# Expert tables of 208 rows, and layer two of six experts with stationary weights

## The chip, the core and the metric

The kernel runs on one core of a Trainium2 chip. Time is device microseconds of one execution. The kernel before takes 768.36 us (median of three runs, 767.66 to 768.78). Engines: TensorE (PE, with weight loads shown apart as PEld), VectorE (DVE), ScalarE (ACT), GpSimd (POOL) and SyncE (SP), which issues most transfers.

## The reference, cut to what matters

Three layers follow each other: masked attention, a dense gated layer, and a routed layer. The change touches only the routed one:

```python
def _moe2_ref(x, w_skip, w_gate, w1, w2):       # x: 2304 tokens x 512
    do_compute = x @ w_skip > 0
    out = x.copy()
    xc = x[do_compute]
    logits = xc @ w_gate                        # 8 experts
    e_idx = np.argmax(logits, axis=1)
    gate_w = softmax(logits)[chosen]
    for e in range(8):
        mask = e_idx == e
        h = np.maximum(xc[mask] @ w1[e], 0.0)   # 512 -> 1024
        y[mask] = gate_w[mask, None] * (h @ w2[e])   # 1024 -> 512
    out[do_compute] = xc + y
```

## The kernel before

Attention, the dense layer (lines 541 to 592 hold most of its matmuls) and the routing fill the first 560 us or so. The routing writes every token row to `out` and scatters the rows of the chosen tokens into a table in DRAM, `xs`, which has SLOTS rows for each expert. An expert with more tokens would be finished by the pass at line 1395, a loop over 128 further rows whose bounds are read from the counts. Expert 0 has its first HEAD = 128 rows processed early: when the tokens of the last two units are ranked, its count is lifted to 128 at least (line 945).

Precision: float32 values are split into a high part (rounded to the engine's fp32r form) and a low part (the rest). A product is high x high + high x low + low x high, each a matmul that runs in fp32r.

All instructions of the span are issued in the order in which the program writes them; each engine runs its own in that order and waits by semaphores. For each of experts 1 to 7 (loop at line 1365):

1. `fetch` issues the loads of the next expert's table rows, `grab` one load of its weights. Weights come in eight pieces of 512 KB (four of w1, four of w2) through a pool of four raw buffers. A `settle` flushes the low part that the piece before left to do, issues a load, and casts a piece on ACT (line 1053). The low part of a w1 piece is POOL's, of a w2 piece DVE's (line 1054; expert 1's pieces alternate). A raw buffer is free, and its next load can be issued, once both parts are made.
2. Hidden stage: eight blocks f, `hidden_wide`. The weights are stationary (128 x 128), the moving side is the token rows transposed, high and low side by side: 448 columns for the high weights, 224 for the low ones, four such pairs a block, into one PSUM bank. Then ACT copies the second half to SBUF (line 1271), DVE adds it to the first (1273), and one block later ACT makes the relu's high part (1277) and DVE its low part (1281). Blocks take banks X and Y in turn, three of each. After every odd block stands a `settle`.
3. `prep` turns the next expert's rows with eight PE transposes (line 1110), in two parts of 128 and SLOTS - 128 rows, each in an X bank, and ACT and DVE make high and low parts (1112, 1114).
4. Layer two: `outputs` once for each part. The tokens are now stationary (128 or 96 columns) and w2 moves, 512 columns, 24 matmuls for a part (lines 1295, 1296, 1300, 1304), into one of two Z banks. DVE multiplies the bank with the gate and adds the row (1306), and POOL scatters the rows to `out` (1307). Two `settle`s stand in each part.

Of the kernel before, what the change touches and what calls it, by code (L numbers as in the profile page):

```python
# [10 lines left out]
F32R = mybir.dt.float32r  # L11
# [3 lines left out]
ALU = mybir.AluOpType  # L15
# [6 lines left out]
def kernel(  # L22
# [14 lines left out]
    nc = tc.nc  # L37
    B, H, S, D = q.shape
    NT, DM = out.shape
# [5 lines left out]
    KD = DM // 128  # L45
# [3 lines left out]
    NF = F // 128  # L49
    WQ = 96  # L50
    NW = S // WQ
    TW = DM + NE + 1
    SLOTS = 224
    HEAD = 128
    RB = 128
    UT = 384
# [30 lines left out]
    def temp(name):  # L87
        return keep.tile([128, UT], F32, tag="t", bufs=NT1, name=name)
# [3 lines left out]

    xs = dram.tile([NE * SLOTS, TW], F32, name="xs")
    vcm = dram.tile([B, S, 4 * D], F32, name="vcm")
# [6 lines left out]
    ident = const.tile([128, 128], F32, name="ident")  # L101
# [13 lines left out]
    def late_consts(i):  # L115
# [12 lines left out]
        if i == KD + 1:  # L128
            nc.gpsimd.iota(desc, pattern=[[-1, NE]], base=NE, channel_multiplier=0, allow_small_or_imprecise_dtypes=True)
            nc.gpsimd.iota(e_off, pattern=[[SLOTS, NE]], base=-int(OOB), channel_multiplier=0, allow_small_or_imprecise_dtypes=True)  # L130
            nc.gpsimd.memset(base_e, 0.0)
# [7 lines left out]
    def bank(shape, tag):  # L139
        return psum[0].tile(shape, F32, tag=tag, bufs=psum[1][tag], name="ps" + tag)  # L140
# [781 lines left out]
    def slab2(shape, dt, name):  # L922
        return late.tile(shape, dt, tag="slab2", bufs=NSLAB2, name=name)
# [133 lines left out]
    after_act = []  # L1057

    def flush(jobs):
        todo = list(jobs)  # L1060
        jobs.clear()
        for job in todo:
            job()

    w_e0, pp = [], []
# [10 lines left out]

    PARTS = ((0, HEAD), (HEAD, SLOTS))

# [22 lines left out]
    def prep(e, xg, parts=PARTS, xx=None, tag="X", gates=True, warm=0):  # L1101
        if xx is None:
            xx = [slab2([128, 2, 2, SLOTS], F32R, f"xx{e}{i}") for i in range(2)]
            xx.append(small.tile([128, 2, 2], F32, tag="gw", bufs=2, name="gw"))
        for a, c in parts:
            t, n = a // HEAD, c - a
            pt = bank([128, KD, n], tag)
            spin(warm, pt)
            for kk in range(KD):
                nc.tensor.transpose(pt[:, kk, :], xg[t][:n, 128 * kk:128 * kk + 128], ident[:n, :n])  # L1110
            for i in range(2):
                nc.scalar.copy(xx[i][:, :, 0, a:c], pt[:, 2 * i:2 * i + 2, :])
            for i in range(2):
                nc.vector.tensor_tensor(
                    xx[i][:, :, 1, a:c], pt[:, 2 * i:2 * i + 2, :], xx[i][:, :, 0, a:c].bitcast(F32), op=ALU.subtract)
            if gates:
                gate(xg, xx, a, c)
        return xx
# [79 lines left out]
    for u in range(NU):  # L1198
        po = [bank([128, UT], "X") for d in range(KD)]
        for f in range(NC):  # L1200
            i = u * NC + f
            ahead(i)
            for d in range(KD):
                ds_ = slice(128 * d, 128 * d + 128)
# [12 lines left out]
    pending, jobs = [], []  # L1217
    xg = head["xg"]

    def hidden(f, w, xx, hts, a=0, c=SLOTS, warm=0):  # L1220
        if f % 4 == 0 and len(hts) <= f // 4:
            hts.append([slab2([128, 4, SLOTS], F32R, f"h{n}{f}") for n in "hl"])
        n = c - a
        ph = bank([128, 2, n], "Y")
        spin(warm, ph)
        fs = slice(128 * f, 128 * f + 128)
        for kk in range(KD):
            xk = xx[kk // 2][:, kk % 2]
            nc.tensor.matmul(ph, lhsT=w[kk][0][:, fs], rhs=xk[:, :, a:c], start=(kk == 0), stop=(kk == KD - 1))
            if kk + 1 < KD:  # L1230
                nc.tensor.matmul(ph[:, 0, :], lhsT=w[kk][1][:, fs], rhs=xk[:, 0, a:c], start=False, stop=False)
            if kk + 2 == KD:
                nc.tensor.matmul(
                    ph[:, 0, :], lhsT=w[kk + 1][1][:, fs], rhs=xx[1][:, 1, 0, a:c], start=False, stop=False)
        hh, hl = (x[:, f % 4, a:c] for x in hts[f // 4])

        def evict():
            flush(pending)
            hs = temp("hs")[:, 0:n]
            nc.scalar.copy(hs, ph[:, 1, :])  # L1240
            flush(jobs)
            nc.vector.tensor_tensor(hs, hs, ph[:, 0, :], op=ALU.add)

            def finish():
                nc.scalar.activation(hh, hs, AF.Relu)
                jobs.append(low_part)

            def low_part():
                nc.vector.scalar_tensor_tensor(
                    hl, in0=hs, scalar=0.0, in1=hh.bitcast(F32), op0=ALU.max, op1=ALU.subtract)  # L1250

            pending.append(finish)

        return evict

    def hidden_wide(f, w, xx, hts):
        if f % 4 == 0:
            hts.append([slab2([128, 4, SLOTS], F32R, f"h{n}{f}") for n in "hl"])
        ph = bank([128, 2, SLOTS], "XY"[f % 2])
        total, rest = ph[:, 0, :], ph[:, 1, :]  # L1260
        fs = slice(128 * f, 128 * f + 128)
        for kk in range(KD):
            xk = xx[kk // 2][:, kk % 2]
            if kk == KD - 1:
                nc.tensor.matmul(total, lhsT=w[kk][1][:, fs], rhs=xk[:, 0, :], start=False, stop=False)
            nc.tensor.matmul(ph, lhsT=w[kk][0][:, fs], rhs=xk, start=(kk == 0), stop=(kk == KD - 1))
            if kk < KD - 1:
                nc.tensor.matmul(total, lhsT=w[kk][1][:, fs], rhs=xk[:, 0, :], start=False, stop=False)
        hh, hl = (x[:, f % 4, :] for x in hts[f // 4])
        hs = temp("hs")[:, 0:SLOTS]  # L1270
        nc.scalar.copy(hs, rest)
        flush(pending)
        nc.vector.tensor_tensor(total, total, hs, op=ALU.add)
        flush(jobs)

        def finish():
            nc.scalar.activation(hh, total, AF.Relu)
            jobs.append(low_part)

        def low_part():  # L1280
            nc.vector.scalar_tensor_tensor(
                hl, in0=total, scalar=0.0, in1=hh.bitcast(F32), op0=ALU.max, op1=ALU.subtract)

        pending.append(finish)

    def outputs(a, c, w, hts, xg, xx, between):
        t, n = a // HEAD, c - a
        flush(pending)
        flush(jobs)
        py = bank([n, DM], "Z")  # L1290
        hl_w2 = []
        for f in range(NF):
            hh, hl = (x[:, f % 4, a:c] for x in hts[f // 4])
            w2h, w2l = (x[:, f % 2, :] for x in w[4 + f // 2])
            nc.tensor.matmul(py, lhsT=hh, rhs=w2h, start=(f == 0), stop=False)
            nc.tensor.matmul(py, lhsT=hh, rhs=w2l, start=False, stop=False)
            hl_w2.append((hl, w2h))
            if f > 1:
                x, y = hl_w2.pop(0)
                nc.tensor.matmul(py, lhsT=x, rhs=y, start=False, stop=False)  # L1300
            if f in (2, 5):
                between()
        for x, y in hl_w2:
            nc.tensor.matmul(py, lhsT=x, rhs=y, start=False, stop=(y is w2h))
        y = xg[t][:n, 0:DM]
        nc.vector.scalar_tensor_tensor(y, in0=py, scalar=xx[2][:n, t, 1:2], in1=y, op0=ALU.mult, op1=ALU.add)
        nc.gpsimd.indirect_dma_start(  # L1307
            out=out[:, :], out_offset=bass.IndirectOffsetOnAxis(ap=xg[t][:n, TW - 1:TW].bitcast(I32), axis=0),
            in_=y, in_offset=None, bounds_check=NT - 1, oob_is_err=False,
        )  # L1310

    w = w_e0
    more, raws_e, wn, hts = True, [], [], []
# [14 lines left out]
    nxt = 1  # L1328
# [22 lines left out]
    xgn = fetch(1)[0]  # L1351
    outputs(0, HEAD, w, hts, xg, pp, idle)
    prep(0, xg, PARTS[1:], pp, warm=6)
    for f in range(NF):
        hidden(f, w, pp, hts, HEAD, SLOTS, 0 if f else 8)()
        if f == 5:
            ppn = prep(1, xgn)
# [4 lines left out]
        settle()  # L1362
    flush(after_act)
    w, xg, pp = wn, xgn, ppn
    for e in range(1, NE):
        nxt = e + 1
        more = nxt < NE
        raws_e, wn, hts = [], [], []
        if more:
            xgn = fetch(nxt)[0]  # L1370
        grab()
        for f in range(NF):
            hidden_wide(f, w, pp, hts)
            if f % 2:
                settle()
        ppn = prep(nxt, xgn) if more else None
        for a, c in PARTS:
            outputs(a, c, w, hts, xg, pp, settle)
        flush(after_act)
        if more:  # L1380
            w, xg, pp = wn, xgn, ppn
    manual.__exit__(None, None, None)

    cnt = const.tile([1, 1], F32, name="cnt")
# [10 lines left out]
    with tc.For_i(SLOTS, top, 128):  # L1395
# [32 lines left out]
        for e in range(NE):  # L1428
# [21 lines left out]
            for kk in range(KD):  # L1450
                t = slab([128, F], F32, f"ow1{e}{kk}")
# [3 lines left out]
            for i in range(NF // 2):  # L1455
                t = slab([128, 2, DM], F32, f"ow2{e}{i}")
# [3 lines left out]
            for f in range(NF):  # L1460
                ph = bank([128, 128], "Y")
                for kk in range(KD):
                    nc.tensor.matmul(
                        ph, lhsT=w1[kk][:, 128 * f:128 * f + 128], rhs=xT[:, kk, :], start=(kk == 0), stop=(kk == KD - 1)
                    )
                nc.scalar.activation(hT[:, f, :], ph, AF.Relu)
            py = bank([128, DM], "Z")
# [36 lines left out]
```

## Time and profile before

| | us |
|---|---|
| median of the runs | 768.36 |
| the profiled execution | 770.95 |
| its span, first to last instruction | 769.2 |
| PE busy | 738.8 (96%) |
| DVE busy | 505.7 (66%) |
| ACT busy | 400.3 (52%) |
| POOL busy | 210.4 (27%) |

Matmuls overlap in the records: one starts before the end of the one before it. So what a matmul costs a busy PE is the distance to the next start, and not its own duration.

### The profile page before, as it was taken

To read this page: it belongs to the slowest core of one execution; us is meant where nothing else is said; L and a number is where in the kernel's file an instruction comes from. 1 tells how busy PE (TensorE), PEld (TensorE's weight loads), DVE (VectorE), ACT (ScalarE), POOL (GpSimd) and SP (SyncE) were. 2 spreads that over 40 slices of the span, in tenths; PEclk is the share of its full clock that TensorE was granted. 3 is DMA by queue.
4 is the path that set the end of the run, shared out by engine and by line. 5 is a ranking of instruction groups with operands and counts; after the bars stand their busy time and mean duration, and the time that the engine had idled before them with its cause. 6 is when DMAs were issued, how large, how long until landed. Compare 5 with 4: busy or idle time off the path is not lost. (4 is left out here: it accounts for less than half of the span.)

```text
span 769.2 us, 13922 instructions
## 1 busy us (share of the span) xinstructions
PE 738.8 (96%) x4773; PEld 674.8 (88%) x4773; DVE 505.7 (66%) x1169; ACT 400.3 (52%) x1123; POOL 210.4 (27%) x233
## 2 busy tenths in 40 slices
PE   8899998999999999999999999999999999999993
PEld 5666766899999999999999999999999888888882
DVE  4599998789877777888764244345554666656550
ACT  5678886745444444444363233244444665567630
POOL 6468778000000000000010020120213755556510
PEclk9999999999999999999999999999989999999997
DMA  7888530063443344434383943536633667776600
GB/s 170 215 195 208 142 91 29 32 199 105 143 153 129 134 135 147 153 119 141 120 292 125 297 137 124 189 113 216 222 132 122 215 235 263 233 237 205 219 19 15
DMA packets 116309, 122.50 MB, mean 159 GB/s; under 512 B 58679, under 2 KB 91191, under 8 KB 116232
## 3 DMA queue, kind: packets, MB, share of 16 engines
q1 hardware_dynamic: 110504, 109.88, 46.1%
q0 software_dynamic: 4000, 8.51, 3.1%
q10 hardware_dynamic: 1728, 3.15, 1.1%
q8 instruction: 40, 0.66, 0.4%
q14 instruction: 37, 0.30, 0.1%
HBM read 90.78 MB, written 36.59 MB: 166 GB/s over the span
## 5 line engine op out<-in xcount | busy, mean ns | idle before, releaser
L541 PE MATMUL psX<-gt,wo 128*128 128x384 f32 x288 | 98.4, 342 | 1.0 <-DVE sl L1127 1.0
L542 PE MATMUL psX<-gt,wo 128*128 128x384 f32 x288 | 96.5, 335 | 0.1
L543 PE MATMUL psX<-gt,wo 128*128 128x384 f32 x288 | 96.4, 335 | 0.0
L592 POOL DMA_DIRECT2D gt<-sC x3 | 1.7, 566 | 256.4 <-DVE sC L590 256.4
L295 ACT ACTIVATE sm<-psX,mx 96x128 f32<-96x128 f32 (+2 forms) x176 | 62.0, 376 | 17.1 <-DVE mx L289 15.1
L308 POOL TENSOR_TENSOR sm<-sm,rs 96x384 f32<-96x384 f32 (+2 forms) x64 | 54.7, 873 | 38.5 <-DVE rs L302 26.7
L587 DVE TENSOR_TENSOR u<-psD,u 128x384 f32<-128x384 f32 x70 | 38.8, 554 | 29.0 <-PE psD L543 27.4
L541 PEld LDWEIGHTS psX<-gt,wo 128*128 128x128 f32 x288 | 54.2, 188 | 1.3 <-DVE sl L1127 1.3
L542 PEld LDWEIGHTS psX<-gt,wo 128*128 128x128 f32 x288 | 54.2, 188 | 0.4 <-DVE gt L857 0.4
L543 PEld LDWEIGHTS psX<-gt,wo 128*128 128x128 f32 x288 | 54.1, 188 | 0.0
L543 PE MATMUL psA<-xhB,wl 128*128 128x384 f32 x140 | 47.0, 336 | 0.7 <-DVE wl L514 0.7
L543 PE MATMUL psD<-xhT,wl 128*128 128x384 f32 x140 | 47.0, 336 | 0.3 <-DVE wl L514 0.3
L541 PE MATMUL psD<-xhT,wh 128*128 128x384 f32 x140 | 46.8, 335 | 0.0
L542 PE MATMUL psD<-xlT,wh 128*128 128x384 f32 x140 | 46.8, 334 | 0.0
L542 PE MATMUL psA<-xlB,wh 128*128 128x384 f32 x140 | 46.8, 334 | 0.0
L541 PE MATMUL psA<-xhB,wh 128*128 128x384 f32 x140 | 46.8, 334 | 0.0
L543 PE MATMUL psB<-xhT,wl 128*128 128x384 f32 x140 | 46.8, 334 | 0.0
L542 PE MATMUL psB<-xlT,wh 128*128 128x384 f32 x140 | 46.8, 334 | 0.0
L541 PE MATMUL psB<-xhT,wh 128*128 128x384 f32 x140 | 46.8, 334 | 0.0
L973 ACT COPY row<-psY 128x256 f32<-128x256 f32 x36 | 13.4, 373 | 62.2 <-PE psY L971 48.2
L974 DVE TENSOR_REDUCE lp<-psY 128x10 f32<-128x40 f32 x36 | 7.2, 200 | 56.6 <-ACT row L973 56.6
L580 ACT COPY psC<-psB 128x384 f32<-128x384 f32 x35 | 16.2, 464 | 51.6 <-PE psB L543 51.6
(764 smaller groups left out, 2263.1 us busy)
## 6 DMA issues: line engine op xcount, KB each, us to landing
w1r<-in_moe_w_dram SPq DMA_DIRECT2D x32, 512.0 KB, 5.2
w2r<-in_moe_w_dram SPq DMA_DIRECT2D x32, 512.0 KB, 3.8
gt<-gt SPq DMA_DIRECT2D x72, 192.0 KB, 3.8
gt<-sC SPq DMA_DIRECT2D x33, 192.0 KB, 2.5
gt<-sA SPq DMA_DIRECT2D x33, 192.0 KB, 1.9
wg<-in_moe_w_gate_dram SPq DMA_DIRECT2D x12, 512.0 KB, 4.0
wv<-in_moe_w_val_dram SPq DMA_DIRECT2D x12, 512.0 KB, 3.7
wo<-in_moe_w_out_dram SPq DMA_DIRECT2D x12, 512.0 KB, 3.8
```

The source lines that it names most:

```text
L295: nc.scalar.activation(sm[:n, w, 0:c], src[:, w, :], AF.Exp, bias=mx[:n, w:w + 1], accum_out=sums[:n, h, w:w + 1])
L308: nc.gpsimd.tensor_tensor(x, x, rs[:n, h, 0:m].rearrange("p (w o) -> p w o", o=1).to_broadcast([n, m, c]), op=ALU.mult)
L541: nc.tensor.matmul(ps, lhsT=whi, rhs=xhi, start=start, stop=False, skip_group_check=skip)
L542: nc.tensor.matmul(ps, lhsT=whi, rhs=xlo, start=False, stop=False, skip_group_check=skip)
L543: nc.tensor.matmul(ps, lhsT=wlo, rhs=xhi, start=False, stop=stop, skip_group_check=skip)
L580: nc.scalar.copy(ps, self.ps[src])
L587: nc.vector.tensor_tensor(self.tm[nm], self.ps["D"], self.tm[nm], op=ALU.add)
L592: eng.dma_start(gts[self.f][2 * self.p + i], self.tm[nm])
L973: nc.scalar.copy(row[m][:, 256 * a:256 * a + 256].rearrange("p (c n) -> p c n", c=2), pr[:, :, 0:128])
L974: nc.vector.tensor_reduce(lp[:, m, a, :], pr[:, :, 128:NR].rearrange("p c (t n) -> p n c t", t=2), axis=AX.XY, op=ALU.add)
```

## The change

SLOTS becomes 208. The parts of a table are then 128 and 80 rows, and the moving sides 416 and 208 columns. The hidden parts are kept differently: one tile for every two blocks holds the high and the low half of each block side by side, where there was a tile of four blocks for each half.

Experts 1 to 6 leave `outputs` for `outputs_wide`. For each quarter d of the 512 outputs, the w2 columns are stationary, high and low tokens move side by side (416 columns for the high weights, 208 for the low ones, eight pairs) into a Z bank; ACT copies the second half, DVE adds the first, and a `settle` follows. The four sums are outputs x tokens; `rows_back` turns them with eight PE transposes into two Y banks, and `store_rows` (the end of the former `outputs`) multiplies, adds and scatters. `rows_back` of an expert is called after block 0 of the next one. In these experts the last relu and low part are issued ahead of `prep`, and no longer behind it. Expert 0 and expert 7 keep `outputs`.

```diff
-    SLOTS = 224
+    SLOTS = 208
...
     def hidden_wide(f, w, xx, hts):
-        if f % 4 == 0:
-            hts.append([slab2([128, 4, SLOTS], F32R, f"h{n}{f}") for n in "hl"])
+        if f % 2 == 0:
+            hts.append(slab2([128, 2, 2, SLOTS], F32R, f"h{f}"))
...
-        hh, hl = (x[:, f % 4, :] for x in hts[f // 4])
+        hh, hl = (hts[f // 2][:, f % 2, i, :] for i in range(2))
...
+        store_rows(a, c, py, xg, xx)
+
+    def store_rows(a, c, py, xg, xx):
+        t, n = a // HEAD, c - a
         y = xg[t][:n, 0:DM]
         nc.vector.scalar_tensor_tensor(y, in0=py, scalar=xx[2][:n, t, 1:2], in1=y, op0=ALU.mult, op1=ALU.add)
         nc.gpsimd.indirect_dma_start(
...
+    def outputs_wide(w, hts, between):
+        ys = []
+        for d in range(KD):
+            ds_ = slice(128 * d, 128 * d + 128)
+            py = bank([128, 2, SLOTS], "Z")
+            total, rest = py[:, 0, :], py[:, 1, :]
+            for f in range(NF):
+                w2h, w2l = (x[:, f % 2, ds_] for x in w[4 + f // 2])
+                h = hts[f // 2][:, f % 2]
+                if f == NF - 1:
+                    nc.tensor.matmul(total, lhsT=w2l, rhs=h[:, 0, :], start=False, stop=False)
+                nc.tensor.matmul(py, lhsT=w2h, rhs=h, start=(f == 0), stop=(f == NF - 1))
+                if f < NF - 1:
+                    nc.tensor.matmul(total, lhsT=w2l, rhs=h[:, 0, :], start=False, stop=False)
+            y = temp("yT")[:, 0:SLOTS]
+            nc.scalar.copy(y, rest)
+            nc.vector.tensor_tensor(y, y, total, op=ALU.add)
+            ys.append(y)
+            between()
+        return ys
+
+    def rows_back(ys, xg, xx):
+        for a, c in PARTS:
+            py = bank([c - a, DM], "Y")
+            for d in range(KD):
+                nc.tensor.transpose(py[:, 128 * d:128 * d + 128], ys[d][:, a:c], ident)
+            store_rows(a, c, py, xg, xx)
...
             hidden_wide(f, w, pp, hts)
+            if f == 0 and left:
+                rows_back(*left)
             if f % 2:
                 settle()
-        ppn = prep(nxt, xgn) if more else None
-        for a, c in PARTS:
-            outputs(a, c, w, hts, xg, pp, settle)
-        flush(after_act)
         if more:
+            flush(pending)
+            flush(jobs)
+            ppn = prep(nxt, xgn)
+            left = outputs_wide(w, hts, settle), xg, pp
+            flush(after_act)
             w, xg, pp = wn, xgn, ppn
+        else:
+            for a, c in PARTS:
+                outputs(a, c, w, hts, xg, pp, settle)
```

## Rows read from the trace of the kernel before

**Rows 1.** The page: busy time of the engines; TensorE's granted clock in 40 slices.
```profile
PE 738.8 (96%) x4773; PEld 674.8 (88%) x4773; DVE 505.7 (66%) x1169; ACT 400.3 (52%) x1123; POOL 210.4 (27%) x233
...
PEclk9999999999999999999999999999989999999997
```

**Rows 2.** Stretches: length, busy time of each engine (instructions), clock, DMA share, GB/s.
```profile
670.60:692.50 21.90, 21.90 (x121) 18.70 (x120) 13.12 (x31) 13.62 (x32) 12.24 (x6) 1.00 0.71 236
```

**Rows 3.** PE in order of time, hidden block 1 of expert 4: start, duration, instruction.
```profile
671.04 0.36 PE L1266 MATMUL psY<-xx,we40h 128*128 128x448 f32 x1
671.23 0.26 PE L1268 MATMUL psY<-xx,we40l 128*128 128x224 f32 x1
671.33 0.38 PE L1266 MATMUL psY<-xx,we41h 128*128 128x448 f32 x1
```

**Rows 4.** PE in order of time: first instructions of the stages of expert 4.
```profile
669.76 0.37 PE L1266 MATMUL psX<-xx,we40h 128*128 128x448 f32 x1
...
679.81 0.93 PE L1110 MATMUL psX<-ident,xg 128*128 128x128 f32 x8
680.52 0.48 PE L1295 MATMUL psZ<-we44h,hh 128*128 128x512 f32 x1
...
686.17 0.39 PE L1295 MATMUL psZ<-we44h,hh 128*96 128x512 f32 x1
...
691.73 0.36 PE L1266 MATMUL psX<-xx,we50h 128*128 128x448 f32 x1
```

**Rows 5.** PE in order of time, expert 0: pairs of 256+128 and 192+96 columns.
```profile
565.98 0.34 PE L1229 MATMUL psY<-xx,we01h 128*128 128x256 f32 x1
...
566.21 0.34 PE L1229 MATMUL psY<-xx,we02h 128*128 128x256 f32 x1
...
589.39 0.32 PE L1229 MATMUL psY<-xx,we01h 128*128 128x192 f32 x1
...
589.62 0.32 PE L1229 MATMUL psY<-xx,we02h 128*128 128x192 f32 x1
```

**Rows 6.** PE in order of time, expert 1: the two turn-backs (brackets: idle before, releaser).
```profile
612.74 0.60 PE L1110 MATMUL psX<-ident,xg 128*128 128x128 f32 x4
614.28 0.55 PE L1110 MATMUL psX<-ident,xg 96*128 96x96 f32 x4 [0.94 <-DVE hl L1281]
```

**Rows 7.** ACT and DVE in order of time, expert 4.
```profile
671.23 0.35 ACT L1271 COPY hs<-psX 128x224 f32<-128x224 f32 x1 [4.32 <-PE psX L1266]
...
680.55 1.05 ACT L1053 CAST we53h<-w1r 128x1024 fp32r<-128x1024 f32 x1
...
688.12 1.05 ACT L1053 CAST we57h<-w2r 128x1024 fp32r<-128x1024 f32 x1 [1.79 <-DMA w2r<-in_moe_w_dram]
...
669.97 0.75 DVE L1306 SCALAR_TENSOR_TENSOR xg<-psZ,gw,xg 96x512 f32<-96x512 f32 x1 [2.55 <-PE psZ L1304]
670.63 1.21 DVE L1054 TENSOR_TENSOR we47l<-w2r,we47h 128x1024 fp32r<-128x1024 f32 x1
671.76 0.39 DVE L1273 TENSOR_TENSOR psX<-psX,hs 128x224 f32<-128x224 f32 x1
```

**Rows 8.** POOL in order of time, and DMA issues (KB each, us to landing).
```profile
674.11 2.40 POOL L1054 TENSOR_TENSOR we50l<-w1r,we50h 128x1024 fp32r<-128x1024 f32 x1 [1.13 <-ACT we50h L1053]
687.40 1.72 POOL L1307 DMA_INDIRECT out_dram<-xg  x1 [3.31 <-DVE xg L1306]
...
w1r<-in_moe_w_dram SPq DMA_DIRECT2D x16, 512.0 KB, 5.3
w2r<-in_moe_w_dram SPq DMA_DIRECT2D x16, 512.0 KB, 3.7
```

**Rows 9.** DVE and ACT in order of time, expert 1.
```profile
613.84 0.38 DVE L1281 SCALAR_TENSOR_TENSOR hl<-psX,hh 128x224 fp32r<-128x224 f32 x1
...
615.63 1.04 ACT L1053 CAST we23h<-w1r 128x1024 fp32r<-128x1024 f32 x1
...
625.39 1.06 ACT L1053 CAST we27h<-w2r 128x1024 fp32r<-128x1024 f32 x1 [2.64 <-DMA w2r<-in_moe_w_dram]
```

More of the change, by code (lines that the diff above doesn't have):

```diff
@@ L1220, in hidden @@
     def hidden(f, w, xx, hts, a=0, c=SLOTS, warm=0):
-        if f % 4 == 0 and len(hts) <= f // 4:
-            hts.append([slab2([128, 4, SLOTS], F32R, f"h{n}{f}") for n in "hl"])
+        if f % 2 == 0 and len(hts) <= f // 2:
+            hts.append(slab2([128, 2, 2, SLOTS], F32R, f"h{f}"))
         n = c - a
@@ L1234, in hidden @@
                     ph[:, 0, :], lhsT=w[kk + 1][1][:, fs], rhs=xx[1][:, 1, 0, a:c], start=False, stop=False)
-        hh, hl = (x[:, f % 4, a:c] for x in hts[f // 4])
+        hh, hl = (hts[f // 2][:, f % 2, i, a:c] for i in range(2))
         def evict():
@@ L1256, in hidden_wide @@
     def hidden_wide(f, w, xx, hts):
-        if f % 4 == 0:
-            hts.append([slab2([128, 4, SLOTS], F32R, f"h{n}{f}") for n in "hl"])
+        if f % 2 == 0:
+            hts.append(slab2([128, 2, 2, SLOTS], F32R, f"h{f}"))
         ph = bank([128, 2, SLOTS], "XY"[f % 2])
@@ L1286, in outputs @@
     def outputs(a, c, w, hts, xg, xx, between):
-        t, n = a // HEAD, c - a
+        n = c - a
         flush(pending)
@@ L1292, in outputs @@
         for f in range(NF):
-            hh, hl = (x[:, f % 4, a:c] for x in hts[f // 4])
+            hh, hl = (hts[f // 2][:, f % 2, i, a:c] for i in range(2))
             w2h, w2l = (x[:, f % 2, :] for x in w[4 + f // 2])
@@ L1364 @@
     w, xg, pp = wn, xgn, ppn
+    left = None
     for e in range(1, NE):
```

## The prediction

> **What bounds the kernel now.** I read the page first: TensorE (PE) is busy for 96% of the span, with 0.9 or more of the clock granted in all slices but two [rows 1]. The table of stretches then says which wait counts in the part that changes, experts 1 to 7: in a whole expert PE is busy in every microsecond at clock 1.00, while VectorE (DVE), ScalarE (ACT) and POOL fill 13.1, 13.6 and 12.2 us of 21.9, and DMA 0.71 of its share [rows 2]. So there the time is the sum of spacings between PE starts, as long as nothing makes PE wait; busy durations overlap and are not to be added. The order-of-time view of PE gives the spacings. In expert 4 the hidden stage runs from 669.76 to 679.81 (10.05 us), eight turn-back transposes to 680.52 (0.71), layer two to 691.73 (11.21): a period of 21.97 us [rows 4].
>
> **Price of a matmul.** One hidden block f lasts 10.05/8 = 1.256 us [rows 4]: four pairs of a 448-column and a 224-column matmul, 314 ns a pair, the wide one near 0.20, the narrow one 0.10 to 0.11 [rows 3]. A pair of 256+128 columns takes 0.23 us, one of 192+96 also 0.23 [rows 5]. So the short ones don't follow their columns: each matmul of new weights costs at least some 0.111 us. The 512-column matmuls of the second output part come every 5.56/24 = 0.2317 us [rows 4], 0.4525 ns a column. "Columns x 0.4525, but 0.111 at least" gives 314 for 448+224 (203+111), 227 for 256+128 and 222 for 192+96, as the rows have it within 8 ns. For 416+208 it gives 188+111 = **300 ns**. Bounds: 291 (the pair in proportion to columns) and 314 (no gain); the straight line between 230 at 384 columns and 314 at 672 also gives 300, which I take.
>
> The Trainium skill, TensorE: Matmul & The Clock Gate, section LDWEIGHTS, says that loading 128 weight columns takes about 128/1.2 = 107 ns, whatever the rows. That speaks against halving the moving side to 208 columns, for the load then outlasts the stream; the trace agrees (0.111 above). By its figure the pair would be an estimated 295 ns and the whole 2 us less than below.
>
> **Part by part**, against the profiled execution (770.95 us, span 769.2; the runs' median is 768.36, 2.6 below it, and I shift by that).
>
> *Rows 224 to 208, hidden stage.* 32 pairs x 14 ns = 0.45 us less per expert, for experts 1 to 7. Expert 0's later part goes from 192+96 to 160+80 columns; since 384 columns and 288 already cost the same, 0. Its fourteen filler matmuls shrink by 6x64 and 8x32 columns, 0 to 0.29 us; I take 0.15. Smaller table fetches and one initial table write fewer lie beside PE work: 0.
>
> *Layer two of experts 1 to 6.* Removed: 48 matmuls, 11.21 us. Added: 4 x 8 pairs x 300 = 9.60, and the 0.09 that the first output matmul costs after transposes (11.21 - 48 x 0.2317). Gain 1.52 (bounds 1.07 and 1.80).
>
> *Transposes back*, eight of 128 moving columns. Four of 128 and four of 96 mixed last 0.93 to their last end, but the next matmul starts 0.71 after them, so 0.22 is overhang [rows 4]. Four of 128 alone last 0.60, four of 96 0.55 [rows 6]: 0.38 and 0.33 without it, which add to the 0.71. So 8 x 0.38/4 = 0.76, with the change of kind **0.85 us** (bounds 0.7 and 1.2), in experts 2 to 7. The existing turn-back saves 0.05 with 80 columns for 96.
>
> *Their wait.* Count t from an expert's first hidden matmul. ACT starts a copy 0.19 us after the next matmul begins (block 1 of expert 4 begins at 671.04, the copy of block 0 at 671.23); the copy takes 0.35, DVE's sum 0.39 [rows 3, 7]. So the last transposed sum is ready at t = 1.0, and hidden block 0 covers PE to t = 1.2. Cover 0.2: cost 0. If ACT or DVE were inside a weight split then (1.05 or 1.21 [rows 7]), it would cost up to 1.0 an expert; by the new order both are free from t = -0.2 on.
>
> *What queues behind it.* DVE then has two weight splits (1.13 each from start to next start, 670.63 to 671.76), block 0's sum (0.3), and both row sums (0.66 each, 669.97 to 670.63) [rows 7]: done at t = 4.9, where before one split and one row sum stood. Block 3 needs the first of the two Y banks back at its start, t = 4.5; it is free at 4.2. Block evictions run 1.5 us late and, at twice 0.35 us of DVE work per 1.2 us block, are in step again by block 4 or 5. POOL gets both scatters ahead of its first low part (1.72 the one in rows 8, two 3.4 at most after the first row sum at t = 4.2; I take 6.7 as their end). Its four low parts (2.40 each [rows 8]) end at 9.1, 11.5, 13.9, 16.3, and with 3.7 us from issue to landing [rows 8] the four w2 loads arrive at 12.8, 15.2, 17.6, 20.0. ACT wants them after the four copies: the stages before layer two end at 9.6 + 0.85 + 0.66 = 11.1, a quarter takes 2.4, the copy follows 0.45 later, so at 14.0, 16.4, 18.8, 21.2: 1.2 us of slack each. Before, the last cast waited 1.79 us for its load [rows 7], which cost nothing because no eviction that PE needs soon stood behind. The w1 loads (5.3 us) of the next expert wait for DVE's w2 low parts, each behind the next quarter's sum, so they start at 18 to 24 and land at 2.5, 4.8, 7.5, 8.7 of it, wanted at 4.1, 6.5, 8.7, 11.1: cost 0.
>
> *Relu and low part of block 7 now come before the turn-back's copies.* They stand behind the w1 cast of 1.05 (680.55): ready 2.3 us after the hidden stage, wanted at 0.8 + 7 x 0.3 = 2.9: cost 0, except in expert 1. There ACT is late from the loads before: the second turn-back waits 0.94 us for a bank that DVE frees at 614.2 [rows 6, 9]. That moment doesn't move, so the 0.45 of the hidden stage is lost; the cast at 615.63 puts block 7's low part at 617.3, PE wants it at 616.9: 0.45 more.
>
> **Sum.** Experts 2 to 6: -0.45 - 1.52 + 0.85 - 0.05 = -1.17 each, -5.85. Expert 1 (no transposes back): -1.52 - 0.05 + 0.45 = -1.1. Expert 7: -0.45 + 0.85 = +0.40. Expert 0: -0.15. Together **-6.7 us**: 770.95 to 764.2 for a profiled execution, 768.36 to **761.7** for the median.
>
> **Rivals.**
> 1. *Columns decide.* A pair costs 291 ns: 416 pairs (7x32 + 6x32) x 8.6 = 3.6 us less, 758.1. For it: a 512-column matmul does scale so. Against: 192+96 costs as much as 256+128. The same page of the Trainium skill, section Back-to-back issue gap, gives N/2.4 + 2.5 ns a matmul, where columns decide; by it 672 columns would be 285 ns, and the trace has 314.
> 2. *The pair stays at 314.* Gain only 1.07 in layer two, none in hidden: five experts at -0.27, expert 1 at -0.67, expert 7 +0.85, expert 0 -0.15: -1.3, 767.0. Against: 384 columns are faster than 672.
> 3. *Slower: ACT's queue.* The four copies stand behind casts that wait for w2 loads, and these for POOL's low parts, now behind two scatters. A load that lands later than its 1.2 us of slack holds ACT and so the next copy; two Z banks hide 2.4 us more. PE waits from 3.6 us of lateness on, and an expert is longer than before from 3.6 + 1.17 = 4.8. Both scatters in full, 7.6 instead of 6.7, a further row sum's delay of 0.7, and loads at 5.3 instead of 3.7 are 3.2 us, and as the next loads wait for the buffers that late casts free, twice that, 6.4: 2.8 - 1.17 = 1.6 us longer in each of five experts, 768.36 + 8.2 - 0.9 for the other three = 776. For it: a 2.64 us wait stood in front of such a cast in expert 1 [rows 9]. Against: POOL is busy 12.2 us of 21.9.
> 4. *The transposes back wait for a split*, 0.7 us each in six experts: 765.9.
> 5. *The change doesn't do what it says:* an expert of over 208 rows starts the overflow pass. The reference's inputs give 116, 130, 185, 196, 145, 194, 136, 99 tokens, and expert 0 ends at row 166 with its head padded to 128. One pass would load 33.5 MB, at 240 GB/s [rows 2] 140 us.
>
> **How the numbers follow.** Forecast 72%, rival 1 8%, rival 2 4%, rival 3 9%, rival 4 6%, rival 5 1%. The forecast's own range is 760 to 764.5: a pair between 296 and 304 gives 1.7 either way, transposes of 0.7 to 1.2 give -0.9 to +2.1. The range 759 to 766.2 adds rival 4 and half of rival 1. About 0.2% (1.5 us) is what a measurement of this kernel can tell from no change: faster 0.86, within it 0.04, slower 0.10.
>
> **What would show it.** Starts of neighbouring hidden blocks 1.20 us apart; layer two of an expert 9.7 us from its first matmul; eight transposes in 0.9 without idle time before them; a period of 20.8 us from expert 2 on; no PE idle but at expert 1's turn-back and block 7. Wrong would be: idle PE before a transpose back or at a bank of layer two behind an ACT cast that waits for DMA (rivals 3, 4), or pairs off 300 ns.

## The result, and the profile after

The changed kernel takes 776.6 us (median of four runs, 774.42 to 777.77) against 768.01 for the kernel before: 1.0103 times as long, 95% interval 1.0078 to 1.0129. The forecast was 761.7, in a range of 759.0 to 766.2. The profiled execution takes 776.8 us, its span 775.1.

The page of the kernel after has PE less busy in a longer span [rows 1], so time went into waiting:

```profile
PE 733.0 (95%) x4917; PEld 683.5 (88%) x4917; DVE 521.4 (67%) x1193; ACT 404.8 (52%) x1147; POOL 204.5 (26%) x233
```

The view of stretches for one expert (length, busy time of PE, PEld, DVE, ACT, POOL, clock, DMA share, GB/s), here expert 5, against [rows 2]:

```profile
691.90:715.20 23.30, 21.54 (x146) 20.73 (x146) 15.72 (x35) 14.16 (x35) 11.37 (x6) 1.00 0.65 213
```

PE, which was busy all through an expert, stands still 1.8 us in it. DMA moves less a microsecond than before (213 GB/s against 236), so it isn't bandwidth that ran out. PE in order of time shows the stages of that expert (against [rows 4]) and where it waits:

```profile
692.92 0.37 PE L1266 MATMUL psX<-xx,we53h 128*128 128x416 f32 x1
693.13 0.49 PE L1342 MATMUL psY<-ident,yT 128*128 128x128 f32 x3
694.21 0.77 PE L1342 MATMUL psY<-ident,yT 128*128 128x128 f32 x5 [0.59 <-DVE yT L1333]
...
698.55 0.46 PE L1266 MATMUL psY<-xx,we50h 128*128 128x416 f32 x1 [1.17 <-DVE xg L1310]
...
699.86 0.35 PE L1266 MATMUL psX<-xx,we50h 128*128 128x416 f32 x1
...
701.06 0.35 PE L1266 MATMUL psY<-xx,we50h 128*128 128x416 f32 x1
```

Two hidden blocks that follow each other start 1.20 us apart (699.86, 701.06): a pair costs 300 ns, as forecast. But the last quarter's sum is late for its transpose (0.59 us), and block 3 waits for the Y bank that DVE's row sum frees late (1.17 us). Experts 2, 3, 4 and 6 also have 0.26 to 0.91 us of idle PE inside layer two, at a Z bank that a late sum frees. ACT and POOL say why. ACT, with the casts of the next expert's w2 (brackets: idle before, and what ended it), against [rows 7]:

```profile
708.02 0.33 ACT L1332 COPY yT<-psZ 128x208 f32<-128x208 f32 x1
710.94 1.06 ACT L1053 CAST we64h<-w2r 128x1024 fp32r<-128x1024 f32 x1 [2.59 <-DMA w2r<-in_moe_w_dram]
711.91 0.32 ACT L1332 COPY yT<-psZ 128x208 f32<-128x208 f32 x1
714.31 1.05 ACT L1053 CAST we65h<-w2r 128x1024 fp32r<-128x1024 f32 x1 [2.09 <-POOL we63l L1054]
715.26 0.33 ACT L1332 COPY yT<-psZ 128x208 f32<-128x208 f32 x1
```

From the second on, each copy of layer two stands behind a cast; the first two of these casts wait 2.59 and 2.09 us for their loads. (The second bracket names a POOL split, which ends at 714.25; the load was issued at 709.58 and landed 4.7 us later, at 714.28.) And POOL, against [rows 8]:

```profile
698.78 1.00 POOL L1311 DMA_INDIRECT out_dram<-xg  x1 [7.65 <-DVE xg L1310]
703.85 0.92 POOL L1311 DMA_INDIRECT out_dram<-xg  x1 [4.08 <-PE psX L1266]
704.79 2.41 POOL L1054 TENSOR_TENSOR we60l<-w1r,we60h 128x1024 fp32r<-128x1024 f32 x1
```

DVE finished both row sums by 699.2, yet the second scatter begins at 703.85. The releaser in the brackets is inferred and wrong: that PE matmul has no part in it. The view of that line, from 698 to 705, has POOL's sequencer in one semaphore wait (count, ns min/median/max), and the view of DMA issues from 698 to 700 has the first scatter's time to landing:

```profile
L1311 POOLq EVENT_SEMAPHORE  x1: 4482/4482/4482, 698.6 to 698.6; - x1
```

```profile
out_dram<-xg POOLq DMA_INDIRECT x1, 4.3
```

Both write `out`, and nothing in the program says that their rows are disjoint: the second carries a wait for the first one's completion. It was there before, too. This is POOL before, at the border of experts 3 and 4, where the second part's row sum was done at about 670.7 [rows 7]:

```profile
665.43 1.72 POOL L1307 DMA_INDIRECT out_dram<-xg  x1 [3.31 <-DVE xg L1306]
672.06 0.92 POOL L1307 DMA_INDIRECT out_dram<-xg  x1 [4.91 <-DVE we47l L1054]
```

The view of that line in the kernel before, from 664 to 674, has the wait (the longer of the two):

```profile
L1307 POOLq EVENT_SEMAPHORE  x2: 17/2997/5977, 665.3 to 665.3; - x2
```

There, one part's rows were ready 5.6 us before the other's, so most of the landing was over when the second rows came. The change makes both ready within 0.7 us.

### The profile page after: what moved, and what is told of

Read it like the earlier page. It is cut to its first block, busy times and chain, and to the rows that moved or that the text cites. A ratio compares the mean times of both kernels' runs of the same rounds, so it can differ in the third digit from the quotient of the medians.

```text
span 775.1 us, 14267 instructions
## 1 busy us (share of the span) xinstructions
PE 733.0 (95%) x4917; PEld 683.5 (88%) x4917; DVE 521.4 (67%) x1193; ACT 404.8 (52%) x1147; POOL 204.5 (26%) x233
```

## The experiments

Theory S: POOL stands in the wait for the first scatter's landing; its low parts of w1 follow late; these hold the raw buffers, so the w2 loads come late; ACT waits in the casts, and the evictions of layer two queue behind them. Rival A: the casts between the copies hold ACT whatever the scatters do. Rival C: splits of weights on DVE and POOL slow each other (DVE's split of the first w2 piece took 2.79 to 3.08 us in experts 2 to 5 of the kernel after and 2.10 in expert 6; the other three took 1.22).

### e1_free: the wait taken away

```diff
-        nc.gpsimd.indirect_dma_start(
+        ins = nc.gpsimd.indirect_dma_start(
             out=out[:, :], ...
         )
+        tc.declare_no_dep(ins.ins, group="rows", reason="disjoint rows")
+        tc.add_to_no_dep_group("rows", ins.ins)
```

> The changed kernel, its scatters to the output declared independent (their rows are disjoint), so that the second of two no longer waits for the first to land. Theory S (POOL stands 4 us in that wait, so the low parts of w1, the w2 loads, ACT's casts and the copies behind them are late): POOL's first low part begins at about 7 us of an expert instead of 9.6, experts 2 to 6 take 20.8 to 21.3 us instead of 22.0 to 24.5, PE stands idle under 2 us in all of them, 763 to 767 us with expert 1's own stall of 2.2 left. Rival A (casts between the copies hold ACT whatever the scatters do, the loads can't come sooner): 773 to 777, casts of w2 still wait 2.6 us and more. Rival C (DVE's and POOL's weight splits slow each other, 2.8 instead of 1.2 us): DVE's splits stay near 2.8, 770 or more.

Measured: 761.83 us, 0.993 of the kernel before (766.82 beside it; ratio 0.9902 to 0.9958). That is 1.2 under the range expected, which left expert 1 its stall of 2.2 us; it was 1.22 in this profile. POOL and ACT in order of time, and the stretch of an expert:

```profile
687.89 0.99 POOL L1311 DMA_INDIRECT out_dram<-xg  x1 [9.12 <-DVE xg L1310]
689.19 0.93 POOL L1311 DMA_INDIRECT out_dram<-xg  x1 [0.31 <-DVE psX L1273]
690.12 2.44 POOL L1054 TENSOR_TENSOR we60l<-w1r,we60h 128x1024 fp32r<-128x1024 f32 x1
```

```profile
697.48 1.05 ACT L1053 CAST we64h<-w2r 128x1024 fp32r<-128x1024 f32 x1
699.65 0.33 ACT L1334 COPY yT<-psZ 128x208 f32<-128x208 f32 x1 [1.12 <-PE psZ L1330]
```

```profile
683.40:704.20 20.80, 20.80 (x145) 20.69 (x145) 13.97 (x34) 14.41 (x36) 11.40 (x6) 1.00 0.71 238
```

The expert begins at 683.41. The first low part stands at 6.7 us of it, where the kernel after has 12.9 (704.79, from 691.92), and 11.75 to 13.54 in its experts 2 to 6, later than the 9.6 in the expectation. No w2 cast of these experts waits for a load, the copy waits for PE, and experts 2 to 6 take 20.85 us each (first hidden matmuls at 620.87, 641.72, 662.57, 683.41, 704.26, 725.11). DVE's splits are all back at 1.2 us. DMA moves 238 GB/s here without a stall. Rival A falls.

### e2_before_free: the same edit on the kernel before

> The kernel before with its scatters declared independent, as a control. Theory S: there a scatter's wait lay beside PE work, so nothing changes: 766.5 to 769.5 us. Rival A: the same. If the waits had a price before, it would be 3 us or more faster.

Measured: 767.17 us, ratio 0.9994 (0.9967 to 1.0021). The wait cost nothing in the old order, though it did hold POOL: without it the second scatter at the border of experts 3 and 4 begins 0.3 us after its row sum (at 668.86), where the kernel before took 1.3.

```profile
669.14 1.65 POOL L1307 DMA_INDIRECT out_dram<-xg  x1 [3.84 <-DVE xg L1306]
```

### e3_rows208: the shorter tables alone

```diff
-    SLOTS = 224
+    SLOTS = 208
```

> The kernel before with tables of 208 rows only. Pairs of 416 and 208 columns at 300 instead of 314 ns save 0.45 us in each of seven experts: 764 to 766 us, no idle PE in experts 2 to 7, periods 21.5. Rival D (the shorter tables by themselves shift expert 0 and 1 so that the splits of DVE and POOL collide): 767 to 771, with idle PE and a lower granted clock in expert 1.

Measured: 763.74 us, ratio 0.9953 (0.9926 to 0.998); five experts of 21.39 to 21.44 us, some 0.55 under the 21.96 of before, where the sum had 0.50, and no idle PE in experts 2 to 7. The time is 0.3 under the range expected. This half of the change does what was forecast, and rival D falls: in this profile DVE's splits of expert 1 take 1.2 us and the clock stays at 1.00 there.

### e4_apart: the scatters apart, the wait kept

```diff
-    def rows_back(ys, xg, xx):
-        for a, c in PARTS:
+    def rows_back(ys, xg, xx, parts=PARTS):
+        for a, c in parts:
...
-            if f == 0 and left:
-                rows_back(*left)
+            if f in (0, 4) and left:
+                rows_back(*left, PARTS[f // 4:f // 4 + 1])
```

> The changed kernel, only the rows of the second part turned back and scattered after hidden block 4 instead of after block 0; the scatter still waits for the one before. Theory S: the wait is hidden by POOL's first low part, experts 2 to 6 take 20.8 to 21.8 us, 763 to 769 in all. Rival A: 773 to 777.

Measured: 761.99 us, ratio 0.9923 (0.9892 to 0.9954), 1.0 under the range expected. POOL now fills the landing with a low part:

```profile
689.11 0.99 POOL L1311 DMA_INDIRECT out_dram<-xg  x1 [8.15 <-DVE xg L1310]
690.12 2.41 POOL L1054 TENSOR_TENSOR we60l<-w1r,we60h 128x1024 fp32r<-128x1024 f32 x1
694.06 0.91 POOL L1311 DMA_INDIRECT out_dram<-xg  x1 [1.53 <-DVE h L1281]
694.99 2.43 POOL L1054 TENSOR_TENSOR we61l<-w1r,we61h 128x1024 fp32r<-128x1024 f32 x1
```

Experts 2 to 4 and 6 take 20.86 us. Here DVE's splits still reach 2 to 3 us in four experts (DVE's groups by form):

```profile
L1054 DVE TENSOR_TENSOR we54l<-w2r,we54h 128x1024 fp32r<-128x1024 f32 x1 | 3.0, 3049 | 0.0
L1054 DVE TENSOR_TENSOR we64l<-w2r,we64h 128x1024 fp32r<-128x1024 f32 x1 | 2.6, 2569 | 0.0
```

and only one expert (21.64, a wait of 0.51) shows a price, though w2 casts wait up to 2.09 us for loads here too. So rival C isn't the main cause: slow splits come with late POOL work and cost little by themselves. When one is slow can be read: in all ten slow splits of the two profiles, the kernel after and e4_apart, DVE's split begins while a POOL split runs and ends 1.08 to 1.10 us after that one's end, nearly the 1.22 that a whole split takes. In e1_free POOL is done with its four before DVE begins.

### e5_together and e8_reversed: the wait in the old order

Both are the kernel before with tables of 208 rows. e5_together put both scatters behind the second part's row sum in the program.

> The kernel before with tables of 208 rows, and both scatters of experts 1 to 6 issued together after the second part, the second waiting for the first to land: the wait of the changed kernel, without the copies of layer two behind ACT's casts. Theory S with its ACT step (the late loads cost because evictions stand behind the casts): 762 to 767 us like e3_rows208, periods 21.4 to 21.6, POOL's first low part 2 to 3 us later in an expert, casts of w2 waiting longer for loads. Rival E (POOL's wait alone is the price, in any order): 770 to 774.

Measured: 763.56 us. It tells nothing: no POOL work stood between the two scatters in the old order, so POOL's own order was as before and the first scatter still ran 6 us ahead of the second (681.70 and 688.05). e8_reversed issues the second part's scatter first:

```diff
-    SLOTS = 224
+    SLOTS = 208
...
-        nc.gpsimd.indirect_dma_start(...)
+        def scatter():
+            nc.gpsimd.indirect_dma_start(...)
+        scatters.insert(0, scatter)
+        if c == SLOTS or not hold[0]:
+            flush(scatters)
...
```

> What e5_together was meant to be: the kernel before with tables of 208 rows, the scatters of experts 1 to 6 issued in the other order, second part first. The first part's scatter, which was issued 5 us sooner, now waits for the second part's to land, so POOL stands about 4 us before its first low part, as in the changed kernel, but layer two has no copies behind ACT's casts. Theory S with its ACT step: POOL's first low part 2.5 us or more later in an expert than in e3_rows208, the w2 casts wait longer for loads, and yet 762.5 to 766 us, periods 21.4 to 21.8. Rival E (POOL's wait alone is the price, in any order): 768 to 774, periods of 22 and more.

Measured: 762.76 us, ratio 0.9941 (0.9917 to 0.9965), periods 21.39 to 21.44. POOL:

```profile
684.67 0.91 POOL L1310 DMA_INDIRECT out_dram<-xg  x1 [4.96 <-DVE xg L1307]
690.01 1.00 POOL L1310 DMA_INDIRECT out_dram<-xg  x1 [4.43 <-DMA out_dram<-xg]
691.03 2.42 POOL L1054 TENSOR_TENSOR we60l<-w1r,we60h 128x1024 fp32r<-128x1024 f32 x1
```

POOL's first low part comes at 7.9 us of the expert (from 683.12), 3.7 later than in e3_rows208 (686.96, from 682.76), and the four w2 casts wait 1.31, 1.01, 1.31 and 1.61 us for loads, where those of e3_rows208 wait 0, 0, 0.78 and 1.46. The time doesn't move: no eviction that PE needs soon stands behind those casts. So the wait by itself has no price in the old order, and rival E falls as far as a lateness of 3.7 us goes. That it became a price through the copies behind the casts is argued from this and from the rows of the kernel after; no run put that kernel's lateness (5.0 us and more) into the old order.

In the kernel after the lateness feeds itself: the late sums hold the row sums, and with them the next scatters. Expert 2, from 622.92, is the first that turns rows back, and shows the wait before any of that:

```profile
627.41 1.00 POOL L1311 DMA_INDIRECT out_dram<-xg  x1 [9.05 <-DVE xg L1310]
633.73 0.92 POOL L1311 DMA_INDIRECT out_dram<-xg  x1 [5.33 <-DVE h L1281]
634.67 2.42 POOL L1054 TENSOR_TENSOR we30l<-w1r,we30h 128x1024 fp32r<-128x1024 f32 x1
```

Its first scatter begins at 4.49 us of the expert, in e1_free at 4.48; the low part begins at 11.75 against 6.73. So the wait makes 5.0 us, and what expert 5 has more (12.9) goes with the feedback.

### e6_free_e1dve and e7_free_again

e7_free_again is e1_free once more, e6_free_e1dve is e1_free with this besides:

```diff
-        eng = nc.gpsimd if e and (i % 2 if e == 1 else i < 4) else nc.vector
+        eng = nc.gpsimd if e and (i % 2 and i < 4 if e == 1 else i < 4) else nc.vector
```

> e1_free with two pieces more of expert 1's weight splits (w2 pieces 5 and 7) on DVE instead of POOL. If DVE's split of piece 6 takes 6.5 us in some executions because POOL splits beside it, that is gone: DVE splits of expert 1's pieces all near 1.2 us, 760 to 762 us, no execution above 765, 0 to 1.5 faster than e7_free_again. If it is no matter: the same as e7_free_again, or slower by the two splits that DVE has more (2.4 us).

> e1_free again, beside the others on the same chip: 761 to 763 us, 4 to 6.5 us under the kernel before.

Measured: 760.84 us (758.35 to 761.29, ratio 0.989, 0.9859 to 0.9922) and 761.73 (761.17 to 762.48, ratio 0.9911, 0.9882 to 0.9941). The first profile has expert 1 at 21.38 us with a wait of 0.59, the second 21.86 with 1.05. Whether e6_free_e1dve removes a DVE split of 6.5 us (last section) is open: the other profile didn't have one either. Its median is the lowest of all versions, but only 0.9 us under that of e7_free_again, and their ranges overlap; both lie under both kernels.

## Why the prediction was wrong

**The step that failed** is the one on what queues behind the transposes: "POOL gets both scatters ahead of its first low part ... I take 6.7 as their end". I counted the scatters' own time on POOL and put the wait that the second carries at nothing. Measured: in expert 2 the first scatter begins at 4.49 us, as forecast (4.2), and the second ends at 11.7; in expert 5 they end at 7.9 and 12.9. With the wait gone (e1_free) the low part does begin at 6.7. The slack of 1.2 us that stood for the w2 loads was then -3.8 in expert 2 and -5 in expert 5, whose first w2 casts waited 3.58 and 2.59 us. Rival 3, which I gave 9%, has the right path from POOL's lateness to PE, and took place. That its 776 is near the 776.6 measured is luck: I let it come from slower scatters and loads, with 7.6 us as the scatters' end, and the real trigger was neither.

**Could it have been read?** Yes. Before, the gap from 665.43 to 672.06 ended 1.3 us after the row sum was done; its row named a DVE split as the releaser, which that scatter doesn't read, and POOL's sequencer stood 5977 ns in one semaphore wait there. A wait whose named releaser can't be the reason was the sign that I passed over.

**The rest of the sum held.** Point by point:
- A pair of 416+208 columns: 300 ns forecast and measured.
- Layer two, transposes, turn-back: expert 4 of e1_free runs from 662.57 to the turn-back at 673.05 in 10.48 us (9.6 + 0.85 forecast), and to 683.41 in 10.36 (0.66 + 9.69). Period 20.85 against 20.80.
- The transposes back wait for nothing in e1_free, as forecast; in the kernel after they wait 0.36 to 0.61 us in four experts, for the late sums.
- Expert 1: 22.0 us forecast and in e1_free, with 1.22 us idle at the turn-back. The kernel after took 24.1 there (last section).
- Expert 7: PE's work ends 21.7 us after its start in e1_free and 21.3 before: +0.4, as forecast. The kernel after has 22.7.
- Experts 1 to 6 together: 132.9 us before, 126.0 forecast, 126.25 in e1_free, 140.8 in the kernel after. Of the 14.54 us between the last two, 12.47 lie in experts 2 to 6 and go with the wait. The other 2.07 lie in expert 1, where the profile of the kernel after has a long DVE split and a lower clock (last section); the long split came without the wait too, in e2_before_free, so these are not shown to be the wait's. How much of the 14.9 us between forecast and median they make is open, since only one execution was profiled.

The profiled executions differ by 5.9 us and the medians by 8.6. The one before had PE at the 1.2 GHz level for a while in expert 0 (granted clock 0.51 from 570 to 580), and the one after did not, though PE was idle 0.84 us of the 5 from 565 to 570 in both. e2_before_free has the old code at clock 1.00 there and begins expert 1 at 598.70, where the kernel before began it at 602.71; so this isn't the change's.

## What to carry to other kernels

Before moving two transfers next to each other, list every wait that each carries, and the one on the transfer before it through a shared destination above all: its price is the landing time, not the issue time, and it hides as long as the two are far apart. An eviction that is put behind another job on an in-order engine inherits all the lateness of that job's inputs; a wait that was free is then a cost. If the rows are disjoint, say so to the scheduler (e1_free), or put other work of the same engine between the two (e4_apart).

## What the runs showed that I had not expected

DVE's split of a w2 piece in expert 1 (128x1024) takes 1.23 us in some executions and 6.49 in others, though in the two shown here the starts agree within 0.1 us on each engine. In the long case POOL's splits beside it keep their 2.4 us, in the short one POOL's first is 2.82. The kernel after has the long one (DVE, then POOL):

```profile
600.74 6.49 DVE L1054 TENSOR_TENSOR we16l<-w2r,we16h 128x1024 fp32r<-128x1024 f32 x1 [0.60 <-ACT we16h L1053]
```

```profile
601.35 2.44 POOL L1054 TENSOR_TENSOR we15l<-w2r,we15h 128x1024 fp32r<-128x1024 f32 x1
603.71 2.43 POOL L1054 TENSOR_TENSOR we17l<-w2r,we17h 128x1024 fp32r<-128x1024 f32 x1
```

and e1_free the short one:

```profile
600.70 1.23 DVE L1054 TENSOR_TENSOR we16l<-w2r,we16h 128x1024 fp32r<-128x1024 f32 x1 [0.56 <-ACT we16h L1053]
```

```profile
601.35 2.82 POOL L1054 TENSOR_TENSOR we15l<-w2r,we15h 128x1024 fp32r<-128x1024 f32 x1
```

The long one ends at 607.23, 1.09 us after POOL's second split (606.14), as the slow splits of the later experts do after theirs; here it began before POOL's first. e2_before_free has it too (6.45), so it isn't the new layer two's. In these two profiles POOL's split begins 0.60 and 0.61 us after DVE's, in the seven short cases with POOL beside it 0.65 to 0.83; whether that decides it, no run tested. In the kernel after, PE then stood idle for 2.16 us, until 608.36, and soon ran at 1.2 GHz, the lower of its two clock levels (clock 0.50):

```profile
609.00:612.00 3.00, 3.00 (x13) 2.92 (x12) 2.15 (x8) 3.00 (x10) 3.00 (x2) 0.50 0.81 321
```

A similar idle in e2_before_free (1.97 us, until 608.35) was followed by clock 1.00 from 609 to 612.
